# Attention followed by a mixture of attention experts: four of six head pairs' partial sums taken ahead for the projections of the last two batches

## The chip, the cores and the metric

The kernel runs on one core of one Trainium2 chip. The metric is device time in microseconds of one execution, the median of several runs. Before the change three runs gave 306.2, 306.74 and 307.45 us.

A core has engines that work side by side, each on its own queue in order: TensorE (PE: matmuls and transposes; its weight loads are shown as PEld), VectorE (DVE), ScalarE (ACT), GpSimd (POOL) and SyncE (SP, which here issues nearly all DMAs). Matmul results land in PSUM, eight banks of 512 f32 per partition, and another engine has to move them to SBUF.

## What is computed

Two layers follow each other. The first is softmax attention with a soft cap, 8 batches, 12 heads, 448 positions, head size 64:

```
scores = scale * q @ k.T
scores = cap * tanh(scores / cap)        # cap = 30
attn   = softmax(scores)
out    = attn @ v                        # 12 heads side by side: x, 768 columns
```

The second takes x (8 x 448 x 768) and runs four causal attention experts, of which each position uses two:

```
logits = x @ w_gate                      # 4 experts; the best two, softmax over their logits
for e in range(4):
    q, k, v = x @ wq[e], x @ wk[e], x @ wv[e]      # 64 columns each
    a   = softmax(causal(scale * q @ k.T))
    out += weight[e] * (a @ v @ wo[e])   # weight 0 where e is not chosen
```

## The kernel before, in words

**Tiles.** The twelve heads of a batch are six *pairs*; there are 48 pairs (`HP` = 6 to a batch), numbered p = 0 to 47. A pair's scores lie in two PSUM tiles, X (three banks) and Y (two banks). For each pair ScalarE runs three tanh over them (L840: X, Y1, Y2) and then one big exponential in SBUF (L852), and then goes on to the next pair. Of the last batch (batch 7) only the first 320 positions (`W1`) are done pair by pair; the other 128 positions of its six pairs are put together in two more steps, 48 and 49. So there are 50 steps. Batch 7's steps are therefore shorter than the earlier ones.

**From a pair to x.** TensorE multiplies the exponentials with V (L867 and L875 in `pv`), VectorE divides by the row sum (L896, L899, tile xk), and the result is transposed into xT, either by TensorE and a VectorE copy (L920, L929) or, from pair 36 on, by a DMA transpose (`turned`, L395). xT[b] has six parts of 128 rows, one for each pair of the batch.

**The experts of a batch.** When a batch's six parts of xT are there, `b_v` multiplies them with the V and gate weights (L989, 260 columns, four position groups n, six matmuls each, one for each pair), and VectorE copies logits (L998, tile lg) and V (L1001, tile vB). `b_qk` does the same for keys and queries (L1016, two groups of two experts, r = 0 and 1). From the logits GpSimd finds the chosen experts in a chain of small steps (`b_gate`, L1056 to L1069, tile ms) and spreads them as a mask (L1112, tile mB). From batch 4 on (`MD`) the mask is transposed by DMA (tile mT) and VectorE multiplies the queries with it (L1034, tile qm). Each of the two choices s = 0 and 1 then has scores (`b_score`, L1156, in the banks of X), one exponential of 1024 columns on ScalarE (L1165, tile pP), a causal cut on GpSimd (L1175, L1182), a product with V (`b_pv`, L1215, L1228, L1230, tile oB), a sum of both choices on GpSimd (`b_ot`, L1240, tile oS), a transpose, and the output projection (`b_wo`, L1277, copied to ob and stored).

The two exponentials of batch b stand in ScalarE's order in steps 6(b+1)+5 and 6(b+1)+6 (`XOFF` = (5, 6)): behind the big exponential of the step before. For batch 6 these are steps 47 and 48.

**The last batch.** `last` does batch 7's first 320 positions: four groups of six matmuls for k and q (L1379, 320 columns), with the gate's logits in between (L1387), V (L1408), scores and exponentials (L1427, L1437), the product with V (L1465), `normed` and the output projection (L1343). `pv2` (L946 to L973) and `last2` (L1525 to L1583) do the same for the remaining 128 positions, which come from the steps 48 and 49. `gate_tail` has the gate's small operations, among them an exponential of 12 columns on ScalarE (L1508).

**What sets the order.** Nothing is issued as it stands in the text. Each operation is recorded in a graph (`G.op`) with its engine, an estimated duration, what it reads and writes, and for some a due time relative to a ScalarE step. `Graph.solve` then plays the graph through with these estimates and picks for each engine, whenever it is free, the ready operation with the earliest due time, shifted by small random amounts (`SEEDS`, `JIT`); groups that go through PSUM get a bank from the list that they name (`AUX` are three banks of their own, `XB` and `YB` those of X and Y). The result is one fixed order for each engine. ScalarE's tanh and exponentials are a fixed chain (`fixed=True`). `evac` lets the planner choose VectorE or ScalarE for a copy, but ScalarE only once its fixed chain is through. Matmuls of a constant tile (`fill`, `NFILL` and `KEEP`) are put in to keep TensorE busy.

Of the kernel before, what the change touches and what calls it, by code (L numbers as in the profile page):

```python
# [19 lines left out]
LAND = 3.672  # L20
LAND0 = 2.314
FLIGHT = 8
JIT = 1.311
SEEDS = (0, 0, 462, 42, 0, 0, 848, 875, 631, 747, 944, 508, 0, 157, 0, 451, 317, 0, 0, 263, 942, 466, 0, 323, 179, 428, 996, 522, 22, 0, 0, 688, 216, 360, 755, 0, 184, 766, 0, 878, 0, 0, 193, 491, 257, 999, 0, 0, 0, 0, 0, 46, 344, 791, 0, 247, 0, 975, 0, 115, 0, 910, 522, 30, 881, 955, 210, 710, 0, 0, 686, 106, 982, 50, 688, 176, 30, 348)
# [4 lines left out]
KEEPN = 2  # L29
HEAD = 12.0  # L30
# [3 lines left out]
NFILL = 46  # L34
# [19 lines left out]
class Graph:  # L54
# [79 lines left out]
    def solve(self, when, banks, lent):  # L134
# [44 lines left out]
        while len(order) < n:  # L179
            best = None  # L180
            for e, rs in ready.items():
# [8 lines left out]
                def rank(x):  # L190
                    u = x[1]
                    if u.name[:4] == "gexp":
                        return -INF, 0.0, 0
                    d = u.due + lag if u.first or left < TAIL else max(u.due + lag, t0 + 0.148)
                    d -= 7.381 * (u.grp is not None and not u.opens and left >= TAIL)
# [3 lines left out]
                    return d - 9.88 * (u.half == 1 and half == 1), u.due, u.idx  # L199

                near = t0 + (0.022 if left >= TAIL else SWITCH + 0.02)
                t, o = min((x for x in c if x[0] <= near), key=rank)
                early = e == "POOL" and t < HEAD
                if (e in ("PE", "DVE") or early) and not o.first:
                    for t2, u in c:
                        if u.first and u.due + lag < t + o.occ + 0.047 and t2 < t + (
                                o.occ if early else max(SWITCH + 0.01, min(o.occ, 0.25))):
                            t, o = t2, u
                            break
# [66 lines left out]
def kernel(  # L276
# [82 lines left out]
    def bank(g):  # L359
        return BANK[g.bank]  # L360
# [93 lines left out]
    eul = sb("eul", [128, 4, 1], f32)  # L454
    slL = sb("slL", [128, 4, E], f32)
# [371 lines left out]
    late = {}  # L827
# [152 lines left out]

    def b_v(b, ref):
        x = b % 2
        for n in range(4):
            g = Group(AUX + XB, 1.8)
            w = WIN[n]
            for j0 in (0, 2, 4):
                def mm(g=g, w=w, j0=j0):
                    for j in (j0, j0 + 1):
                        nc.tensor.matmul(  # L989
                            bank(g)[:, 0 : E * Dh + E], xT[x][:, j, w : w + 128], wvg[:, j, :],  # L990
                            start=(j == 0), stop=(j == NDC - 1),
                        )

                pe(0, mm, [("xT", x, j) for j in range(NDC)] + [("wvg", e) for e in range(E + 1)],
                   [("vps", b, n)], g, occ=0.22, name=f"v{b}_{n}",
                   due=(ref, 3.171 + 1.4 * n))
            lo = 64 if n == 3 else 0
            dve(0.08, lambda g=g, n=n: nc.vector.tensor_copy(  # L998
                lg[x][:, (n + 1) % 4, :], bank(g)[:, E * Dh : E * Dh + E]),
                [("vps", b, n)], [("lg", x, n)], g)  # L1000
            dve(c_dve(E * Dh), lambda g=g, n=n, lo=lo: nc.vector.tensor_copy(  # L1001
                vB[x][lo:128, n, :, 0:Dh],
                bank(g)[lo:128, 0 : E * Dh].rearrange("p (e d) -> p e d", d=Dh)),
                [("vps", b, n)], [("vB", x, n)], g, name=f"vB{b}")

    def b_qk(b, ref):
        x = b % 2
        for r in range(2):
            for which in "kq":
                g = Group(AUX + XB, 2.4)  # L1010
                w2 = (wq2 if which == "q" else wk2)[r]
                for j in range(NDC):
                    def mm(g=g, w2=w2, j=j, which=which):
                        for o, t in ((0, slice(0, S)),) if which == "k" else (
                                (0, slice(KM, S)), (TL, slice(0, KM))):
                            nc.tensor.matmul(  # L1016
                                bank(g)[:, o : o + t.stop - t.start], w2[:, j, :],
                                xT[x][:, j, t], start=(j == 0 and o == 0), stop=(j == NDC - 1),
                                skip_group_check=True)

                    pe(S, mm, ([("mB", 0), ("mB", 1)] if which == "q" and b >= MD else []) + [("xT", x, i) for i in range(NDC)] + [
                            (f"w{which}2", 2 * r), (f"w{which}2", 2 * r + 1)],
                        [(which, b, r)], g, name=f"{which}{b}_{r}",
                        due=(ref, 22.258 + 3.706 * r + 9.535 * (which == "q")))
                if which == "k":
                    dve(c_dve(S), lambda g=g, r=r: nc.vector.tensor_copy(
                        kB[x][r], bank(g)[:, 0:S]), [("k", b, r)], [("kB", x, r)], g, name=f"kB{b}")
                    continue
                if b < MD:
                    dve(c_dve(S), lambda g=g, r=r: nc.vector.tensor_copy(  # L1030
                        qB[x][r], bank(g)[:, 0:S]), [("q", b, r)], [("qB", x, r)], g, name=f"qB{b}")
                    continue
# [232 lines left out]
    def b_wo(b, ref, off, step=1.0):  # L1265
        x = b % 2
        for n in range(4 if b < LB - 1 else 3):
# [3 lines left out]
            for f in range(2):  # L1271
                g = Group(AUX + XB if b < LB - 1 else AUX, 1.6)
# [91 lines left out]
    def last(ref):  # L1364
# [9 lines left out]
        for r in range(2):  # L1374
            for which in "kq":
                g = Group(ANY, 2.4)
                w_ = (wq2 if which == "q" else wk2)[r]
                for j in range(NDC):
                    pe(W1, lambda g=g, w_=w_, j=j: nc.tensor.matmul(  # L1379
                        bank(g)[:, 0:W1], w_[:, j, :], xT[x][:, j, 0:W1], start=(j == 0),  # L1380
                        stop=(j == NDC - 1), skip_group_check=True),
                        xr + [(f"w{which}2", 2 * r), (f"w{which}2", 2 * r + 1)],
                        [(which, b, r)], g, name=f"{which}L{r}_{j}")
                    if which == "q" and r == 0:
                        def lgt(g=g, j=j):
                            for n in range(3):
                                nc.tensor.matmul(  # L1387
                                    bank(g)[:, W1 + E * n : W1 + E * (n + 1)],
                                    xT[x][:, j, WIN1[n] : WIN1[n] + 128], wvg[:, j, E * Dh :],
                                    start=False, stop=(j == NDC - 1), skip_group_check=True)  # L1390

                        pe(0, lgt, xr + [("wvg", E)], [("q", b, 0)], g, occ=0.09, name="lgL")
# [61 lines left out]
        for n in range(3):  # L1454
# [5 lines left out]
            def mm(g=g, n=n):  # L1460
                for e in range(E):
# [11 lines left out]
                   [(b, 3, "z")]), None, WIN1[n], (ref, 11.607))  # L1473
# [45 lines left out]
    def last2(ref):  # L1519
# [67 lines left out]
        for e in range(E):  # L1587
# [3 lines left out]
               gt2[3][:, 1, 0], W1, (ref, 11.726))  # L1591
# [15 lines left out]
    for p in range(NPV):  # L1607
# [13 lines left out]
        for what in order:  # L1621
            if what == "Y2" and p:
# [4 lines left out]
                xt(p - 1, (ACTS["Y1", p], 4.099))  # L1627
# [91 lines left out]
```

## Time and profile before

| what | value |
|---|---|
| median of three runs | 306.74 us |
| the profiled execution, its own time | 306.68 us |
| its span, first to last instruction | 304.9 us |
| mean granted TensorE clock | 0.996 |
| PE busy | 281.0 us (92%) |
| DVE busy | 213.8 us (70%) |
| ACT busy | 290.5 us (95%) |
| POOL busy | 184.4 us (60%) |
| last tanh or big exponential ends | 285.08 us |

A row of a timeline gives the start in us from the span's beginning, the duration, the engine, the source line, the operation, output <- inputs with their shapes, how many instructions were merged (x3), and in brackets the engine's idle time before it with what ended that. In a merged row of TensorE the time goes from the first start to the last end; matmuls overlap, since the next begins while the one before drains. A due time or an estimate in the code is the planner's, not a measurement.

### The profile page before, as it was taken

What the parts mean: (1) busy time and instruction counts of PE and PEld (TensorE: products, weight loads), DVE (VectorE), ACT (ScalarE), POOL (GpSimd) and SP (SyncE); (2) the same over time, 40 slices, a digit from 0 to 9 for tenths busy, and PEclk for the clock granted to TensorE, in tenths of its full rate; (3) what the DMA queues carried; (4) which work ended last, traced back from release to release, by engine and by line L of the source; (5) the groups of instructions that cost most, each with busy time, mean ns of one, the idle gap of its engine ahead of it and who ended that gap; (6) DMA issues with size and microseconds to landing.
All of it is one profiled execution on the core that took longest, in us unless ns stands there. A gap on an engine that the chain in (4) does not pass through costs nothing.

```text
span 304.9 us, 9009 instructions
## 1 busy us (share of the span) xinstructions
PE 281.0 (92%) x3499; PEld 188.9 (62%) x3499; DVE 213.8 (70%) x646; ACT 290.5 (95%) x245; POOL 184.4 (60%) x515
## 2 busy tenths in 40 slices
PE   8988789999999999999999999989999999999993
PEld 4554456676765776667665677656665666567751
DVE  3344557766777877777876878688876867588783
ACT  5999999999999999999999999999999999999572
POOL 6882253998699586855689473945677312932230
PEclk9999999999999999999999999999999999999998
DMA  6789989998983699769984973259038820655127
GB/s 180 173 202 246 241 200 297 254 248 218 257 199 117 196 260 228 189 180 271 246 217 121 256 210 114 37 155 218 3 69 105 251 53 19 56 149 133 37 113 251
DMA packets 86875, 53.13 MB, mean 174 GB/s; under 512 B 47536, under 2 KB 83120, under 8 KB 86832
## 3 DMA queue, kind: packets, MB, share of 16 engines
q1 hardware_dynamic: 86448, 52.13, 68.5%
q8 instruction: 27, 0.44, 0.7%
q10 hardware_dynamic: 384, 0.43, 0.4%
q14 instruction: 16, 0.13, 0.2%
HBM read 36.19 MB, written 11.01 MB: 155 GB/s over the span
## 4 chain that ended last, share of the span: by engine, by line
ACT 48%; PE 35%; DVE 6%; POOL 5%; issue 3%; DMA 3%; ACTq 0%; POOLq 0%; DVEq 0%
ACT yp L840 25%; ACT yp L852 20%; PE A L875 4%; PE Y L787 4%; PE A L1016 4%; PE X L1156 3%; PE A L1277 3%; PE A L867 2%; PE A L989 2%; ACT pP L1165 2%; DMA vf<-in_v_dram 1%; PE A L691 1%; PE X L787 1%; DMA ktf<-in_k_dram 1%; PE X L797 1%
## 5 line engine op out<-in xcount | busy, mean ns | idle before, releaser
L852 ACT ACTIVATE yp<-yp 128x3136 f16<-128x3136 f16 (+4 forms) x51 | 140.5, 2758 | 0.0
L840 ACT ACTIVATE yp<-Y 128x896 f16<-128x896 f32 (+2 forms) x100 | 97.8, 978 | 1.2 <-PE Y L787 1.2
L840 ACT ACTIVATE yp<-X 128x1344 f16<-128x1344 f32 (+2 forms) x50 | 66.5, 1330 | 0.2
L875 PE MATMUL A<-v,yp 128*128 128x65 f16 x1116 | 55.3, 193 | 0.0
L875 PEld LDWEIGHTS <-yp 128*128 128x128 f16 x1116 | 48.4, 97 | 5.1 <-issue 3.6
L867 PE MATMUL A<-vtz,yp 128*128 128x130 f16 x186 | 41.3, 222 | 5.5 <-ACT yp L852 3.3
L899 DVE TENSOR_TENSOR xk<-A,rca 128x256 f16<-128x256 f32 (+1 forms) x96 | 39.6, 415 | 2.8
L896 DVE RECIPROCAL rca<-A 128x4 f32<-128x4 f32 (+1 forms) x96 | 17.0, 178 | 27.8 <-PE A L875 26.3
L641 POOL CAST q<-qf 112x512 f16<-112x512 f32 x44 | 26.7, 617 | 9.4 <-PE A L691 7.9
L677 POOL CAST v<-vf 128x384 f16<-128x384 f32 x48 | 24.3, 514 | 12.6 <-PE A L875 9.0
L383 DVE COPY ob<-A 128x384 f32<-128x384 f32 (+1 forms) x51 | 27.0, 552 | 4.6 <-PE A L1277 4.1
L867 PEld LDWEIGHTS <-yp 128*128 128x128 f16 x186 | 18.0, 97 | 18.8 <-issue 8.9
L626 POOL CAST k<-kf 128x384 f16<-128x384 f32 x33 | 16.5, 514 | 18.2 <-DMA kf<-in_k_dram 10.6
L787 PE MATMUL Y<-qk 64*128 64x448 f16 x136 | 24.7, 358 | 2.2 <-ACT yp L840 1.9
L1230 DVE SCALAR_TENSOR_TENSOR oB<-A,rcb,mw 128x256 f16<-128x256 f32 x53 | 24.8, 480 | 1.4 <-DVE rcb L1228 0.2
L750 DVE COPY qk<-A 128x960 f16<-128x960 f16 x32 | 20.7, 653 | 6.4 <-PE A L691 6.0
L1277 PE MATMUL A<-wo,oT 128*128 128x384 f16 x108 | 23.9, 326 | 1.1 <-DVE xT L929 0.5
L1215 PE MATMUL A<-vB,pP 128*128 128x260 f16 x134 | 22.1, 274 | 0.9 <-DVE qk L750 0.4
L989 PE MATMUL A<-wvg,xT 128*128 128x260 f16 x168 | 20.8, 274 | 0.2 <-DVE xT L929 0.2
L1016 PE MATMUL A<-xT,wk 128*128 128x448 f16 x84 | 20.0, 353 | 0.3 <-DVE oB L1230 0.2
L1016 PE MATMUL A<-xT,wq 128*128 128x64 f16 (+1 forms) x168 | 20.2, 260 | 0.0
L691 PE MATMUL A<-ident,q 112*128 112x112 f16 x192 | 19.2, 214 | 1.0 <-DVE oB L1230 0.4
(231 smaller groups left out, 582.1 us busy)
## 6 DMA issues: line engine op xcount, KB each, us to landing
qf<-in_q_dram SPq DMA_DIRECT2D x23, 448.0 KB, 6.2
kf<-in_k_dram SPq DMA_DIRECT2D x23, 384.0 KB, 5.4
vf<-in_v_dram SPq DMA_DIRECT2D x23, 384.0 KB, 5.6
out_dram<-ob SPq DMA_DIRECT2D x21, 384.0 KB, 3.4
ktf<-in_k_dram SPq DMA_DIRECT2D x46, 32.0 KB, 4.9
vtf<-in_v_dram SPq DMA_DIRECT2D x46, 32.0 KB, 4.7
out_dram<-ob SPq DMA_DIRECT2D x6, 192.0 KB, 3.1
ob<-in_moe_wv_dram SPq DMA_DIRECT2D x2, 384.0 KB, 4.7
```

Of the source, the lines that this page charges most:

```text
L383: (nc.scalar.copy if o.eng == "ACT" else nc.vector.tensor_copy)(dst(), src())
L641: e(q16[i], qf[s][:, h].rearrange("p h (c d) -> p c h d", c=QC))
L787: nc.tensor.matmul(dst[:, g, o], kT[r, 128 * (c + 1) : 128 * (c + 2)], t[r, qs], start=True, stop=True,)
L840: ACTS[what, p] = act(c_act(n * (b - a)), lambda: nc.scalar.activation(y[:, a:b, 0:n], src[:, 0 : b - a, 0:n], AF.Tanh, scale=isc / capf), ...
L852: act(c_act(n * (b - a), False), lambda a=a, b=b, n=n: nc.scalar.activation(y[:, a:b, 0:n], y[:, a:b, 0:n], AF.Exp, scale=capf), ks, ks, f ...
L867: nc.tensor.matmul(ps[:, n, :, :], y[:, 2 * S + w : 2 * S + w + 128], vtz[u], start=(n == 0), stop=False, skip_group_check=True,)
L875: nc.tensor.matmul(ps[:, n, h, :], y[:, o : o + 128], v16[u][:, h, c, :], start=False, stop=(c == 2), skip_group_check=True,)
L899: dve(c_dve(128 * m), lambda g=g, i=i, rc=rc, m=m: nc.vector.tensor_tensor(xk[p % NXK][:, 2 * i : 2 * i + m, :, :], view(g)[:, 0:m, :, 0:D ...
L989: nc.tensor.matmul(bank(g)[:, 0 : E * Dh + E], xT[x][:, j, w : w + 128], wvg[:, j, :], start=(j == 0), stop=(j == NDC - 1),)
L1016: nc.tensor.matmul(bank(g)[:, o : o + t.stop - t.start], w2[:, j, :], xT[x][:, j, t], start=(j == 0 and o == 0), stop=(j == NDC - 1), skip ...
L1230: dve(c_dve(E * Dh) + 0.06, lambda g=g, k_=k_, n=n: nc.vector.scalar_tensor_tensor(oB[s][:, n, :, :], view(g)[:, :, 0:Dh], rcb[k_][:, 0, : ...
L1277: nc.tensor.matmul(bank(g)[:, 0 : D // 2], oT[x][:, n // 2, r, n % 2, :], wo2[r][:, c0:c1], start=(r == 0), stop=(r == 1),)
```

## The change

For the last two batches, the sums over the first four of the six pairs are formed as soon as these four pairs are there, copied to SBUF as f32, and added again when the sum over the other two pairs is evacuated.

- Batch 6 (`LB - 1`): the new function `b_half`, called in step 40 (6 x 6 + 4, when the pairs 36 to 39 are through), forms partial sums for the four groups of V and logits and for the keys of r = 0. `b_v` and `b_qk` then run over the last two pairs only, and VectorE adds (`plus`) instead of copying. The other three key and query groups of batch 6 stay as they were.
- Batch 7: in `last`, each of the four groups for k and q is split in a group over four pairs (bank from `AUX`) with a copy to SBUF, and a group over two pairs, whose evacuation is an addition on VectorE. The logits' matmuls of the first four pairs stand behind the fifth pair's projection.
- `late`: batch 6's two exponentials stand in steps 46 and 47 instead of 47 and 48.
- Output projections of batch 6 may use X's banks too, and their due times move.
- The planner's constants, seeds and due times are new, and 35 instead of 46 short warm-up matmuls are issued.

```diff
-NFILL = 46
+NFILL = 35
+LDUE = 7.797
+LSTEP = 0.74
+PJ = 4
+PDUE = 2.793
+PSTEP = 11.594
...
-    late = {}
+    late = {LB - 1: (4, 5)}
...
+    def plus(b, key, out, src, part):
+
+        if b < LB - 1 or key not in half:
+            return nc.vector.tensor_copy(out, src)
+        return nc.vector.tensor_tensor(out, src, part(half[key]), ALU.add)
...
+    def b_half(b, ref):
+
+        x = b % 2
+        xr = [("xT", x, j) for j in range(PJ)]
+        for i in range(4):
+            n = (0, 3, 1, 2)[i]
+            g = Group(AUX + XB, 1.8)
+            for j0 in range(0, PJ, 2):
+                pe(0, lambda g=g, n=n, j0=j0: v_mm(g, x, n, range(j0, min(j0 + 2, PJ)), 0, PJ - 1),
...
+            dve(c_dve(E * Dh + E), lambda g=g, n=n: nc.vector.tensor_copy(
+                half["v", n], bank(g)[:, 0 : E * Dh + E]), [("hp", "v", n)], [("half", "v", n)], g,
+                name="hv")
+        for i, (which, r) in enumerate((("k", 0),)):
...
     def b_v(b, ref):
         x = b % 2
+        j1 = PJ if b == LB - 1 else 0
...
         for r in range(2):
             for which in "kq":
-                g = Group(ANY, 2.4)
                 w_ = (wq2 if which == "q" else wk2)[r]
-                for j in range(NDC):
+                h = (which, r)
+                g = Group(AUX, 2.4)
+                for j in range(PJ):
                     pe(W1, lambda g=g, w_=w_, j=j: nc.tensor.matmul(
                         bank(g)[:, 0:W1], w_[:, j, :], xT[x][:, j, 0:W1], start=(j == 0),
+                        stop=(j == PJ - 1), skip_group_check=True),
...
+                dve(c_dve(W1), lambda g=g, h=h: nc.vector.tensor_copy(
+                    halfL[h], bank(g)[:, 0:W1]), [("hpL",) + h],
+                    [("halfL",) + h] + halfL_w[h], g, name=f"h{which}L")
+                g = Group(ANY, 2.4)
+                for j in range(PJ, NDC):
...
-                evac(W1, lambda dst=dst: dst[:, 0:W1], lambda g=g: bank(g)[:, 0:W1],
-                     [(which, b, r)], [(f"{which}B", x, r)], g, name=f"{which}Bl")
+                dve(c_dve(W1), lambda dst=dst, g=g, h=h: nc.vector.tensor_tensor(
+                    dst[:, 0:W1], bank(g)[:, 0:W1], halfL[h], ALU.add),
+                    [(which, b, r), ("halfL",) + h], [(f"{which}B", x, r)], g, name=f"{which}Bl")
...
+                if p == HP * (LB - 1) + PJ:
+                    b_half(LB - 1, ACTS["Y1", p])
...
-                        b_wo(bb, ACTS["Y1", p], *((22.656, 1.8) if bb < LB - 1 else (16.715, 0.5)))
+                        b_wo(bb, ACTS["Y1", p], *((21.59, 1.8) if bb < LB - 1 else (21.884, 0.5)))
```

More of the change, by code (lines that the diff above doesn't have):

```diff
@@ L997, in b_v @@
-            lo = 64 if n == 3 else 0
[L998 to L1004, printed above, removed]
+            hr = [("half", "v", n)] if b == LB - 1 else []
@@ L1010, in b_qk @@
                 g = Group(AUX + XB, 2.4)
-                w2 = (wq2 if which == "q" else wk2)[r]
-                for j in range(NDC):
[L1013 to L1031, printed above, removed]
+                soon = b == LB - 1 and (which, r) in half
```

119 lines of the change are left out of this document (88 added, 31 removed).

## The prediction

> **What bounds the kernel now.** I read the page's head first, then busy time by stretches, then ScalarE's timeline at the end. The columns of a stretch are PE, PEld, DVE, ACT and POOL (busy us, with instruction counts), the granted TensorE clock, the DMA share and GB/s.
>
> ```profile
> span 304.9 us, 9009 instructions
> ...
> 50.00:100.00 50.00, 48.57 (x627) 33.09 (x628) 36.58 (x106) 49.96 (x37) 44.53 (x118) 1.00 0.89 223
> ...
> 270.00:275.00 5.00, 5.00 (x84) 3.66 (x82) 4.03 (x13) 5.00 (x6) 1.36 (x5) 1.00 0.43 124
> 275.00:280.00 5.00, 4.98 (x69) 3.50 (x67) 4.27 (x17) 5.00 (x6) 0.76 (x2) 1.00 0.75 198
> 280.00:285.00 5.00, 4.99 (x78) 3.79 (x77) 4.76 (x21) 5.00 (x5) 2.26 (x2) 1.00 0.18 30
> 285.00:290.00 5.00, 4.94 (x76) 3.80 (x74) 3.62 (x16) 1.74 (x7) 0.36 (x2) 1.00 0.12 26
> 290.00:295.00 5.00, 4.57 (x54) 3.03 (x54) 4.18 (x17) 4.35 (x11) 2.97 (x8) 1.00 0.17 70
> 295.00:300.00 5.00, 4.67 (x51) 2.49 (x47) 4.53 (x16) 3.30 (x9) 0.00 (x0) 1.00 0.65 259
> ```
>
> ```profile
> 264.75 2.24 ACT L852 ACTIVATE yp<-yp 128x2240 f16<-128x2240 f16 x1
> 266.70 0.88 ACT L840 ACTIVATE yp<-Y 128x640 f16<-128x640 f32 x1
> ...
> 268.73 2.27 ACT L852 ACTIVATE yp<-yp 128x2240 f16<-128x2240 f16 x1
> 270.74 1.17 ACT L1165 ACTIVATE pP<-X 128x1024 f16<-128x1024 f32 x1
> ...
> 276.02 1.08 ACT L1165 ACTIVATE pP<-X 128x1024 f16<-128x1024 f32 x1
> ...
> 282.36 0.30 ACT L1508 ACTIVATE gt<-gt 128x12 f32<-128x12 f32 x1
> 282.46 2.62 ACT L852 ACTIVATE yp<-yp 128x1920 f16<-128x1920 f16 x2
> 287.12 0.43 ACT L383 CAST qB<-X0s 128x320 f16<-128x320 f32 x1 [2.04 <-PE X0s L1379]
> ...
> 300.41 0.52 ACTq L1358 DMA_DIRECT2D out_dram<-kf  x1
> ```
>
> The reader sees two stages. As far as 285.08 us (282.46 + 2.62) ScalarE sets the time: 49.96 of 50 us busy in one stretch, 5.00 of 5 from 270 to 285. Work taken from another engine there gives nothing; a wait put before a ScalarE instruction costs its full length. Behind 285.08 comes the tail, 19.8 us to the span's end, in which ScalarE waits (2.04 us for one projection of the last batch). TensorE is full from 270 to 290 and at 4.57 and 4.67 of 5 afterwards, VectorE at 4.18 and 4.53. What leaves TensorE's queue after about 280 us should therefore shorten the tail, unless VectorE is late.
>
> **Term 1: TensorE's work behind the last scores.** The last scores of the attention start at 279.71. I compare the planned queues behind them in both programs.
>
> ```profile
> 278.12 0.64 PE L1215 MATMUL A<-vB,pP 128*128 128x260 f16 x4
> 278.78 0.33 PE L920 MATMUL A<-ident,xk 128*128 128x128 f16 x3
> 278.95 0.27 PE L1215 MATMUL X2s<-vB,pP 128*128 128x260 f16 x1
> ...
> 279.71 0.34 PE L787 MATMUL Y<-qk,kd 64*128 64x128 f16 x6
> ...
> 282.64 0.57 PE L1379 MATMUL A<-xT,wk 128*128 128x320 f16 x3
> ...
> 283.31 0.30 PE L1379 MATMUL A<-xT,wk 128*128 128x320 f16 x1
> ```
>
> One 320-column matmul takes 0.30 from start to end and three take 0.57, so each further one holds the queue (0.57 - 0.30)/2 = 0.135 us; for 260 columns it is (0.64 - 0.27)/3 = 0.12. Before, 24 projections k and q of batch 7 stand behind the last scores; after, 8 do, the other 16 (four pairs in each of four groups) standing in front: -16 x 0.135 = -2.16. But nine matmuls of batch 6's attention times V stand there instead of three (+6 x 0.12 = +0.72), and the three transposes of pair 47, ahead of the scores before (0.33 with their drain, half taken), come behind them (+0.15). Sum: **-1.29**. If VectorE is what the tail waits for, it is 0; if the nine and the transposes fill holes, -2.16. I take -1.29, as TensorE's 4.94 of 5 is nearest to a full queue. All twelve output projections of batch 6 stay in the tail in both queues, so the earlier exponentials relieve nothing there.
>
> Each of the four new half sums costs a VectorE copy of 128x320, and each later evacuation becomes an addition.
>
> ```profile
> 260.53 0.62 DVE L1026 CAST kB<-A 128x448 f16<-128x448 f32 x1
> ...
> 267.74 0.60 DVE L1034 TENSOR_TENSOR qm<-A,mT 128x448 f16<-128x448 f32 x1
> ...
> 287.26 0.49 DVE L383 CAST kB<-X1s 128x320 f16<-128x320 f32 x1
> ```
>
> An operation on two tensors takes 0.60 where a copy of that width takes 0.62: the additions cost what the copies did. The new copies are 4 x 0.49 = 1.96 us and fall before the last scores, in 270 to 285, where VectorE has 15 - (4.03 + 4.27 + 4.76) = 1.94 us left: hidden, with no reserve. Behind that, two V evacuations and one of the last rows' k go to ScalarE and one q evacuation comes back from it. I cost this at 0, and its lower cover is rival 2. Batch 6's five half copies (four of 260, one of 448 columns) fall near 250 us, where ScalarE is the bound; 0, if no score is late.
>
> **Term 2: the small exponential.** The gate's exponential at 282.36 takes 0.10 in front of the last big one at 282.46. After, it stands behind it: **-0.10**.
>
> **Term 3: batch 6's first exponential has a new wait.** Before, it runs at 270.74. After, it stands behind the big exponential that ends at 266.70, four microseconds sooner. It needs scores, these need the masked queries, these a transposed mask, this the gate, and this the logits.
>
> ```profile
> 255.61 0.31 PE L787 MATMUL Y<-qk,kd 64*128 64x320 f16 x2
> ...
> 255.85 0.84 PE L989 MATMUL A<-wvg,xT 128*128 128x260 f16 x6
> ```
>
> ```profile
> 258.57 0.16 DVE L998 COPY lg<-A 128x4 f32<-128x4 f32 x1
> ...
> 264.26 0.42 DVE L899 TENSOR_TENSOR xk<-A,rca 128x256 f16<-128x256 f32 x1
> ...
> 268.46 1.67 DVE L1034 TENSOR_TENSOR qm<-A,mT 128x448 f16<-128x448 f32 x3
> ```
>
> ```profile
> 258.81 0.29 POOL L1056 TENSOR_TENSOR g_c<-lg 128x64 f32<-128x64 f32 x1 [4.09 <-DVE lg L998]
> ```
>
> ```profile
> 263.04 3.92 SPq L395 DMA_TRANSPOSE mT<-mB  x2
> ```
>
> ```profile
> DMA to landing us min/median/max: 4.3/4.5/4.6
> ```
>
> ```profile
> 269.58 1.06 PE L1156 MATMUL X<-qm,kB 128*128 128x256 f16 x18
> ```
>
> In the new TensorE queue the fourth V projection of batch 6 (now two matmuls) stands right behind the scores that started at 255.61, so at 255.85, the place of the row shown. Two matmuls end 0.39 later, at 256.24. In VectorE's queue one normalisation (0.42 and its reciprocal) stands ahead of the logits: they start near 256.5 and GpSimd's first gate step at 256.75 instead of 258.81, 2.06 sooner. From there to the mask's DMA it was 263.04 - 258.81 = 4.23: issue at 260.98. Landing 4.5 later: 265.48. Two multiplications, the second 0.53 behind the first and 0.60 long: 266.6. The first scores may begin on the first of them; all 18 take 1.06: 267.65 to 267.7. ScalarE is free at 266.70: **+1.0** of idle time, and everything up to the last exponential moves with it.
>
> Bounds: with a landing of 4.3, and the first scores overlapped with the second multiplication, +0.6; with 4.6 and a logits copy later by one V evacuation (0.42), +1.5; 0 if the gate gains two more microseconds, for which I see no reason. Behind the waiting multiplication in VectorE's queue stand the normalisations of pairs 44 and 45 and five copies of batch 5's output; they are 1.5 us later than ScalarE's beat would allow, but VectorE was idle before them (rival 3 is the case where this does not suffice).
>
> The Trainium skill's page "DMA: Bandwidth & Descriptors", section "Latency and other measured facts", gives DMA transposes 261 GB/s; the mask is 256 KB, so the estimate from it would be 1.0 us plus the issue. By that price the mask would land over 2 us sooner and term 3 would be 0, which is rival 1; the trace's 4.3 to 4.6 us disagrees, and I go by it.
>
> **What moves elsewhere.** The new seeds and dues reorder the whole queue, loads included. ScalarE's order is the same up to pair 45. I cost this at 0, since before it hid everything (0.04 us of ScalarE idle in 50 to 100), with up to +1 if one load comes late, and not below zero, as ScalarE has nothing left to gain there. Eleven warm-up matmuls fewer are issued, all behind the first scores, where TensorE waits for ScalarE: 0.
>
> **Sum.** The profiled execution took 306.68 us, 1.78 outside its span, and the three runs have a median of 306.74, so no correction is needed. 306.68 - 1.29 - 0.10 + 1.0 = 306.29: **306.3 us**, no change that can be told. A measurement of this kernel tells about 0.5% (1.53 us) from no change.
>
> **Rivals.**
>
> 1. *No wait at batch 6's exponential.* The mask lands in time and the relief stays: 306.68 - 1.29 - 0.10 = 305.3; with the full 2.16 it is 304.4. For it: the chain to the logits loses two thirds of its matmuls. Against it: the row of 255.61 holds back the fourth projection. Chance 0.25.
> 2. *The relief is not had, because VectorE becomes the tail's bound.* Its stretch of 270 to 285 has 1.94 us free and gets 1.96; the evacuations of the last keys and queries then come late and TensorE idles: 306.68 - 0.10 + 1.0 = 307.6. For it: 4.76 of 5 at 280 to 285. Against it: three evacuations go to ScalarE. Chance 0.17.
> 3. *Slower: a second stall behind the first.* The second mask's transpose stands behind the first in the DMA queue; its products free the bank in which pair 45's attention times V starts, and TensorE's queue has the scores of pair 47 behind that. It decides when the second mask lands over 1.2 us later than the first: the two issues together took 3.92 us in the row above, so the second may start up to 2.6 behind. Then 1.4 us are added to the 1.0, and VectorE, late by 2.4, lets no relief through: 306.68 + 2.4 - 0.10 = 309.0. Against it: the earlier row was held up by two other transposes in front. Chance 0.17.
> 4. *It doesn't do what it says*: the moved sums still wait for the last pairs, and the exponential is not sooner in time. The added copies then cost 0 to 0.5: about 307. Chance 0.03; the new queues do show the four partial groups in front.
>
> **How the numbers follow.** The forecast (305.5 to 307.2) has 0.38, rivals 0.25, 0.17, 0.17, 0.03. Faster than 305.2 are about three quarters of rival 1 and a little of the forecast's lower end: 0.21. Slower than 308.3 are rival 3 and the upper end of rival 2: 0.20. Within: 0.59. The range goes from 304.4 (rival 1 with full relief) to 309.0 (rival 3), leaving out some 0.15; the forecast's own is 305.5 to 307.2.
>
> **What would show it.** Term 3: ScalarE idle of about 1.0 us before the first exponential of batch 6, released by the masked scores, with the multiplication before them waiting for the mask's DMA, and GpSimd's first gate step of batch 6 near 256.7. Term 1: the last big exponential ending near 286.0, and from there 18.5 us to the end instead of 19.8. Rival 1: no idle there. Rival 2: VectorE without gaps from 275 to 290 and TensorE waiting for its evacuations. Rival 3: a second gap before the tanh of pair 47. The forecast is wrong if ScalarE shows idle time before 240 us, which no term contains, or if the tail's length stays at 19.8.

## The result, and the profile after

The changed kernel has a median of 305.07 us (six runs, 304.30 to 305.50), the kernel before one of 307.06 beside it (six runs, 306.20 to 307.45). The ratio is 0.9934, 95% interval 0.9916 to 0.9952: 0.66% or 2.0 us faster, and the interval lies wholly below 1. The forecast was 306.3, no change that can be told; rival 1, no wait at batch 6's exponential, gave 305.3.

The head of the page of the changed kernel, and its busy time by stretches (columns as before):

```profile
span 303.4 us, 8986 instructions
...
270.00:275.00 5.00, 5.00 (x74) 3.75 (x73) 3.71 (x14) 4.62 (x5) 1.62 (x6) 1.00 0.61 202
275.00:280.00 5.00, 5.00 (x67) 3.36 (x66) 4.32 (x12) 5.00 (x6) 0.00 (x0) 1.00 0.11 25
280.00:285.00 5.00, 5.00 (x86) 4.21 (x83) 4.93 (x19) 5.00 (x5) 1.76 (x2) 1.00 0.39 121
285.00:290.00 5.00, 4.97 (x74) 3.77 (x73) 4.65 (x22) 2.55 (x10) 0.96 (x2) 1.00 0.23 52
290.00:295.00 5.00, 4.86 (x66) 2.80 (x61) 4.51 (x19) 4.70 (x14) 2.94 (x8) 1.00 0.21 80
295.00:300.00 5.00, 3.55 (x33) 1.86 (x31) 3.41 (x12) 2.83 (x7) 0.00 (x0) 1.00 0.99 383
```

The two stages are the same. From 270 to 285 ScalarE is still full but for 0.38 us; behind it TensorE stays fuller than before in 290 to 295 (4.86 against 4.57) and falls off sooner (3.55 in the last row against 4.67): the tail's work is denser and ends earlier.

The timeline of the changed kernel along the chain of term 3, then ScalarE at the end of its stage, then the end of the kernel:

```profile
256.56 0.29 POOL L1107 TENSOR_TENSOR g_c<-lg 128x64 f32<-128x64 f32 x1 [5.05 <-DVE lg L999]
260.78 2.72 SPq L400 DMA_TRANSPOSE mT<-mB  x2
263.74 0.62 DVE L1085 TENSOR_TENSOR qm<-A,mT 128x448 f16<-128x448 f32 x1 [1.11 <-PE Y L801]
264.48 2.12 ACT L866 ACTIVATE yp<-yp 128x2240 f16<-128x2240 f16 x1
264.62 0.62 DVE L1085 TENSOR_TENSOR qm<-A,mT 128x448 f16<-128x448 f32 x1 [0.25 <-PE A L1011]
265.25 1.08 PE L1207 MATMUL X<-qm,kB 128*128 128x64 f16 x18
266.44 1.07 ACT L1216 ACTIVATE pP<-X 128x1024 f16<-128x1024 f32 x1
...
273.40 1.13 ACT L854 ACTIVATE yp<-X 128x1152 f16<-128x1152 f32 x1 [0.38 <-PE X L801]
...
279.89 0.34 PE L801 MATMUL Y<-qk,kd 64*128 64x128 f16 x6
...
282.49 2.58 ACT L866 ACTIVATE yp<-yp 128x1920 f16<-128x1920 f16 x2
...
297.75 0.82 PE L1394 MATMUL A<-wo,oTL 128*128 128x384 f16 x4
...
299.12 0.53 ACTq L1409 DMA_DIRECT2D out_dram<-kf  x1
```

```profile
DMA to landing us min/median/max: 2.7/2.8/2.9
```

Batch 6's first exponential runs at 266.44 with no bracket behind it: ScalarE waited for nothing. The gate began at 256.56 and the masks were issued at 260.78, but they landed in 2.7 to 2.9 us, not 4.5. The scores end at 266.33 (265.25 + 1.08), 0.11 us before ScalarE is free. The first multiplication, at 263.74, is put down to a score matmul that it does not read; the mask, issued at 260.78, landed just then (263.65) and is the likelier cause.

For the end, the kernel before has this last matmul (its last scores, its last store and its span stand in the prediction):

```profile
298.92 0.81 PE L1343 MATMUL A<-wo,oTL 128*128 128x384 f16 x4
```

That gives the account of the profiled executions (306.68 and 305.08 us). The last scores start 0.18 later (279.71, 279.89). From there to the end of the last matmul TensorE takes 18.68 instead of 20.02: -1.34. From there to the span's end, one copy and a store, 4.8 instead of 5.2: -0.4. Sum -1.6. ScalarE's last big exponential ends where it did (285.08, 285.07), so the whole gain lies in the tail.

### The profile page after: what moved, and what is told of

The parts are those of the page before. It is cut to its first block, busy times and chain, and to the rows that moved or that the text cites. A ratio compares the mean times of both kernels' runs of the same rounds, so it can differ in the third digit from the quotient of the medians.

```text
span 303.4 us, 8986 instructions
## 1 busy us (share of the span) xinstructions
PE 281.0 (93%) x3488; PEld 187.7 (62%) x3488; DVE 218.2 (72%) x653; ACT 290.8 (96%) x247; POOL 184.7 (61%) x515
## 4 chain that ended last, share of the span: by engine, by line
ACT 59%; PE 30%; issue 3%; DMA 3%; DVE 2%; SPq 1%; POOL 1%; POOLq 0%; ACTq 0%
ACT yp L854 29%; ACT yp L866 25%; PE A L1011 4%; ACT pP L1216 4%; PE A L889 3%; PE Y L801 3%; PE A L1328 3%; DMA kf<-in_k_dram 2%; PE A L1003 2%; PE A L1266 2%; PE A L881 2%; PE X L1207 1%; PE A L934 1%; PE X L801 1%; DMA oT<-oS 1%
## 5 line engine op out<-in xcount | busy, mean ns | idle before, releaser
L854 ACT ACTIVATE yp<-Y 128x896 f16<-128x896 f32 (+2 forms) x100 | 99.2, 992 | 1.2 <-PE Y L801 1.2
L913 DVE TENSOR_TENSOR xk<-A,rca 128x256 f16<-128x256 f32 x96 | 39.9, 415 | 3.2
L388 DVE COPY ob<-A 128x384 f32<-128x384 f32 (+1 forms) x48 | 25.2, 551 | 4.7 <-PE A L1328 4.3
L910 DVE RECIPROCAL rca<-A 128x4 f32<-128x4 f32 x96 | 17.0, 178 | 15.3 <-PE A L889 13.9
L1328 PE MATMUL A<-wo,oT 128*128 128x384 f16 x98 | 22.4, 325 | 1.0 <-DMA oT<-oS 0.5
L1291 POOL TENSOR_TENSOR oS<-oB,oB 128x512 f16<-128x512 f16 x14 | 16.0, 1153 | 10.6 <-issue 9.5
L1003 PE MATMUL A<-wvg,xT 128*128 128x260 f16 x168 | 22.1, 274 | 0.4 <-DVE vB L999 0.3
L705 PE MATMUL A<-ident,q 112*128 112x112 f16 x192 | 19.9, 213 | 1.2 <-POOL q L655 1.1
L1226 POOL TENSOR_SCALAR_AFFINE_SELECT pP<-pP 128x384 f16<-128x384 f16 x14 | 7.4, 525 | 20.6 <-ACT pP L1216 20.6
```

What stands on the lines that cost most here:

```text
L388: (nc.scalar.copy if o.eng == "ACT" else nc.vector.tensor_copy)(dst(), src())
L854: ACTS[what, p] = act(c_act(n * (b - a)), lambda: nc.scalar.activation(y[:, a:b, 0:n], src[:, 0 : b - a, 0:n], AF.Tanh, scale=isc / capf), ...
L913: dve(c_dve(128 * m), lambda g=g, i=i, rc=rc, m=m: nc.vector.tensor_tensor(xk[p % NXK][:, 2 * i : 2 * i + m, :, :], view(g)[:, 0:m, :, 0:D ...
L1003: nc.tensor.matmul(bank(g)[:, 0 : E * Dh + E], xT[x][:, j, WIN[n] : WIN[n] + 128], wvg[:, j, :], start=(j == j1), stop=(j == jn),)
L1328: nc.tensor.matmul(bank(g)[:, 0 : D // 2], oT[x][:, n // 2, r, n % 2, :], wo2[r][:, c0:c1], start=(r == 0), stop=(r == 1),)
```

## Experiments

**Which part of the change makes the gain.** Theory T: the four partial sums of batch 7 shorten the tail. Rival L: the earlier exponentials do. Each of the next four kernels is planned anew after its edit, but with the constants, seeds and due times of the kernel that it is taken from. Its loss therefore holds two things, what the edit does and what constants cost that belong to another kernel, and idle time can come in far from the edit. Whether the new constants alone would change the time of the kernel before was not run.

*Exponentials back in their old places.*

```diff
-    late = {LB - 1: (4, 5)}
+    late = {}
```

> The changed kernel with batch 6's two exponentials back in the places they had before (one pair later each); all partial sums kept. Theory T, the gain is TensorE's work taken out of the tail by batch 7's four partial sums (the trace: 18.70 us from the last scores' start to the last matmul's end against 20.04): still 305.1, within 0.5. Rival L, the earlier exponentials make the gain, since batch 6's attention and output leave the tail earlier: 306.4 to 307.0.

308.63 us, ratio to before 1.0059 (1.0038 to 1.0080): slower than both kernels, and outside what either theory expected. The timeline of this kernel:

```profile
274.19 0.78 PE L1207 MATMUL X<-qm,kB 128*128 128x256 f16 x12
...
275.47 1.25 PE L1431 MATMUL A<-xT,wk 128*128 128x320 f16 x8
276.56 0.71 PE L1431 MATMUL A<-xT,wq 128*128 128x320 f16 x4
...
277.82 0.33 PE L1207 MATMUL X<-qm,kB 128*128 128x128 f16 x4
...
278.25 1.02 ACT L1216 ACTIVATE pP<-X 128x1024 f16<-128x1024 f32 x1 [1.56 <-PE X L1207]
```

Twelve matmuls of the new partial sums (L1431) stand in TensorE's queue between the scores of batch 6's second exponential, and ScalarE idles 1.56 us; another 0.43 is lost at the first exponential. In the tail TensorE takes 19.18 from the last scores, 0.5 more than with the earlier exponentials, as 14 matmuls of batch 6's attention stand there instead of 9. The profiled execution loses another 1.8 from its last matmul to the span's end (6.6 instead of 4.8), which was not followed up. So T as stated falls, and L too: in this plan the partial sums cost ScalarE 2.0 us of idle time, more than the 1.3 that they bring in the tail, and the earlier exponentials clear the stretch in which the sums are taken.

*Batch 7 without its partial sums.*

```diff
-                h = (which, r)
-                g = Group(AUX, 2.4)
-                for j in range(PJ):
...
                 g = Group(ANY, 2.4)
-                for j in range(PJ, NDC):
+                for j in range(NDC):
...
-                dve(c_dve(W1), lambda dst=dst, g=g, h=h: nc.vector.tensor_tensor(
-                    dst[:, 0:W1], bank(g)[:, 0:W1], halfL[h], ALU.add),
+                evac(W1, lambda dst=dst: dst[:, 0:W1], lambda g=g: bank(g)[:, 0:W1],
```

> The changed kernel without batch 7's four partial sums: its k and q projections are whole groups of six matmuls again, evacuated by copies; batch 6's partial sums and the earlier exponentials stay. Theory T: the 16 matmuls of 0.135 us are back behind the last scores, 305.1 + 1.3 to 2.2 = 306.4 to 307.2. Rival L: 305.1, within 0.5.

306.18 us, ratio 0.9986 (0.9966 to 1.0005): of the 0.66% there is 0.14% left, within the interval nothing; by the medians 1.1 us are lost, and the interval does not meet that of the changed kernel (0.9916 to 0.9952). From the last scores to the last matmul TensorE takes 19.76 against 18.68, +1.08; the 16 moved matmuls come back, and fewer of batch 6's attention stand beside them. The whole tail, from the last big exponential to the span's end, is 19.75 against 18.29. ScalarE's stage ended 0.9 sooner in this plan (0.6 of that was there in the first 25 us), which hides part of the loss. T is right in this half: given the earlier exponentials and these constants, the partial sums of batch 7 carry most of the gain.

*Batch 6 without its partial sums.*

```diff
-                if p == HP * (LB - 1) + PJ:
-                    b_half(LB - 1, ACTS["Y1", p])
...
-        j1 = PJ if b == LB - 1 else 0
+        j1 = 0
```

> The changed kernel without batch 6's partial sums: V and k projections whole, earlier exponentials and batch 7's partial sums kept. By the forecast's chain the gate's first step goes back from 256.6 to about 258.8 us, the masks' issue to 263.0; with a landing of 2.8 the scores end near 267.7, with 4.5 near 269.5, against ScalarE free at 266.4: idle time of 1.3 to 3.1 before batch 6's first exponential, 306.4 to 308.2. Rival, the planner finds room by itself and the partial sums of batch 6 buy nothing: 305.1.

*The kernel before with the earlier exponentials alone* (the same one-line edit, the other way round):

> The kernel before with the earlier exponentials alone: no partial sums, old constants. Theory T: the gate of batch 6 is not sooner, so batch 6's first exponential waits 1.3 to 3.1 us and the tail keeps its 19.8: 308.1 to 310.1. Rival L: the tail gets shorter by itself, 306.0 or less. Third: the planner hides both, about 307.

311.63 us (ratio 1.0154, 1.0132 to 1.0175) and 321.83 us (1.0486, 1.0463 to 1.0510), both slower than any theory expected. Without the partial sums of batch 6: an idle time far ahead, the gate's first step, a small operation of the gate on VectorE, and batch 6's first exponential. Then the kernel before, its gate and its exponential:

```profile
176.30 1.02 ACT L1216 ACTIVATE pP<-X 128x1024 f16<-128x1024 f32 x1 [1.30 <-POOL kz L645]
...
259.25 0.29 POOL L1107 TENSOR_TENSOR g_c<-lg 128x64 f32<-128x64 f32 x1 [1.87 <-DVE lg L998]
...
267.08 0.18 DVE L1151 RECIPROCAL g_w<-g_w 128x4 f32<-128x4 f32 x1 [1.41 <-POOL g_w L1143]
...
270.10 1.02 ACT L1216 ACTIVATE pP<-X 128x1024 f16<-128x1024 f32 x1 [1.14 <-PE X L1207]
```

```profile
266.12 0.29 POOL L1056 TENSOR_TENSOR g_c<-lg 128x64 f32<-128x64 f32 x1 [7.71 <-DVE lg L998]
...
279.93 1.02 ACT L1165 ACTIVATE pP<-X 128x1024 f16<-128x1024 f32 x1 [9.27 <-PE X L1156]
```

Without batch 6's partial sums the gate comes at 259.25 instead of 256.56, 2.7 us later. But 2.3 of that is not the gate's: ScalarE itself is that late in this plan (the big exponential of 260.50 starts at 262.82), from idle times at exponentials of earlier batches, 0.80 at 105.16 and 1.30 at 176.30, which the edit does not touch. Measured from ScalarE's beat, the start of its big exponentials, the gate is 0.4 later. The exponential then waits 1.14. That this is near the 1.3 of the forecast's chain is chance: the first mask had landed at 266.19, and VectorE stood until 267.08 at a small operation that GpSimd released, in front of the multiplication. Another 3.4 us are lost in the tail (21.7 from the last big exponential to the end, against 18.3), which was not followed up. So this run does not show what batch 6's partial sums bring.

In the kernel before with the earlier exponentials the gate comes at 266.12 and the wait is 9.27; there too ScalarE was late ahead of it, 3.7 us behind the kernel before. In this plan the earlier exponentials alone are a heavy loss. How much of it due times made for the new places would take away was not run.

**Why the mask landed in 2.8 and not 4.5.** The landings of the other two masked batches in the trace of before, batch 4 and then batch 5, could have been read ahead of the result:

```profile
DMA to landing us min/median/max: 2.7/3.1/3.5
```

```profile
DMA to landing us min/median/max: 4.7/4.8/4.9
```

So both prices were there. The row that the forecast used has one thing beside it. A mask is 1,024 packets of 256 bytes; these are the DMA packets of the 0.7 us in which the first half of batch 6's first mask moved (264.2 to 264.9, before; columns are packets, MB, and their time as a share of 16 engines), and then those of the next 1.6 us (264.9 to 266.5).

```profile
q1 hardware_dynamic: 507, 0.13, 463.8%
q8 instruction: 1, 0.02, 14.5%
...
mT<-mB SPq DMA_TRANSPOSE x2, 4.5
```

```profile
q1 hardware_dynamic: 24, 0.01, 3.7%
```

One packet of 16 KB from an instruction queue starts in the same stretch. The mask's packets that start there are under way for 463% of the engines' time (about 100% in full flow: 98.7% from 264.5 to 265.2 in the kernel before with 84 more instructions, below), and behind them the mask all but stands still: 24 packets in 1.6 us. By its volume that queue is TensorE's:

```profile
PE 281.0 (92%) x3499; PEld 188.9 (62%) x3499; DVE 213.8 (70%) x646; ACT 290.5 (95%) x245; POOL 184.4 (60%) x515
...
q8 instruction: 27, 0.44, 0.7%
```

0.44 MB over 2 x 3499 instructions is 63 bytes each, and 27 packets make one in 259 instructions. Such a packet is called a piece here. Theory F: a transpose whose packets meet such a piece lands late. Rival Q: it lands late because two other transposes stand directly ahead of it in the queue, as they did before and not after. The other masks of the same trace go with F: a piece starts 0.5 us behind the issue of batch 4's first mask (landing 3.5) and 1.2 behind that of batch 5's first (4.9), and none near batch 4's second (2.7). The test moves the pieces and nothing else: some of the 42 early warm-up matmuls of 512 columns (pairs 1 to 7, far ahead of everything here) are cut in two or four, which adds TensorE instructions; the planner still sees one operation each, so the order stays.

```diff
-                    pe(512, lambda g=g: nc.tensor.matmul(
-                        bank(g)[:, 0:512], warm[:, 0:128], warm[:, 0:512], start=True, stop=True),
+                    pe(512, lambda g=g, p=p, k=2: [nc.tensor.matmul(
+                        bank(g)[:, i : i + 512 // k], warm[:, 0:128], warm[:, i : i + 512 // k],
+                        start=True, stop=True) for i in range(0, 512, 512 // k)],
```

*The kernel before with 84 more instructions (k = 2):*

> The kernel before, with the 84 more instructions: the piece that arrived at 265.8 us, in the flight of batch 6's masks (issued 263.04 and 264.36, landed in 4.6 and 4.3), moves to about 262.4, ahead of them; two pair transposes stand in front of the masks as before. Theory F: the masks land in 2.7 to 3.3 us; time unchanged, about 307.0, as no exponential waits for them there. Rival Q: 4.3 to 4.6 as before.

307.04 us, one run. The packets of 264.4 to 267.0, in which both masks moved:

```profile
q1 hardware_dynamic: 2106, 0.52, 89.3%
...
mT<-mB SPq DMA_TRANSPOSE x2, 2.8
```

No instruction packet there, no stuck packets, landing 2.7 to 2.8 with the two transposes still in front. The piece now starts at 260.65, and the first of those two transposes, which it meets, lands in 4.0 us instead of 2.3. Q falls. Batch 5's masks, 4.7 to 4.9 before, landed in 2.7 to 2.8 as well.

*The changed kernel with 84 more (k = 2) and 108 more (k = 4 for pair 7, else 2), and the control with 252 more (k = 4):*

> The changed kernel with each of its 42 early 512-column warm-up matmuls cut into two of 256: 84 more TensorE instructions (matmul and weight load each) far ahead of everything disputed, same order otherwise. TensorE's instruction stream comes in 16 KB pieces, one in about 256 instructions (0.44 MB for 6,976 matmuls and loads); 84 more move the piece that arrived at 266.7 us to about 264.4. Theory F, a transpose whose flight meets such a piece lands late: the second mask of batch 6 (issued 262.15) lands in 4.0 to 4.8 us instead of 2.7, the first still in 2.8 to 2.9; ScalarE has no new idle time, time 305.1. Rival Q, a transpose lands late when others stand directly ahead of it in the queue: the order is the same, so both land in 2.7 to 2.9; time 305.1.

> As the run with 84 more instructions, but six of the 42 matmuls are cut into four: 108 more, and the piece of instructions moves to about 263.0, into the flight of the first mask of batch 6 (issued 260.78). Theory F: the first mask lands in 4.0 to 4.8 us, near 265.3; the multiplications end near 266.4, the scores near 267.4, and ScalarE idles 0.6 to 1.0 before batch 6's first exponential, as the forecast had it: 305.1 + 0.8 = 305.9. Rival Q: landing 2.7 to 2.9, no idle time, 305.1.

> Control: all 42 warm-up matmuls cut into four, 252 more instructions, which is about one whole piece, so the pieces arrive where they did. Theory F: both masks of batch 6 land in 2.7 to 2.9 us, no idle time, 305.1. If the added instructions themselves cost something, or delay the transposes by another way than the place of the pieces, it shows here: over 305.5 or a landing over 3.5. Rival Q: 2.7 to 2.9 too.

304.43 us (ratio 0.9922, 0.9897 to 0.9948), 304.38 (0.9914, 0.9891 to 0.9936) and 305.24 (0.9943, 0.9922 to 0.9964); landings 2.7 to 2.9, 2.7 to 2.8, 2.8 to 3.1. The first two did not test what they were made for. Their expectations took a slow trickle of packets at 266.7 in the changed kernel for the piece, but the trickle follows it; the piece itself came at 265.1, and 84 more instructions brought it to 260.4, ahead of the masks' data. The control put it back at 265.0, as one period should.

*48 more (k = 2 for pairs 1 to 4) and 60 more (pairs 1 to 5), set from the right place:*

> The changed kernel with 24 of its early warm-up matmuls cut in two: 48 more TensorE instructions. In the run with 84 more, the 16 KB piece of TensorE's instructions that came at 265.1 us (by the single packet of the instruction queue) came at 260.4, ahead of the masks' data, so that run did not test what it was made for. 48 more should bring it to about 262.4, while the first mask's packets move (262.0 to 263.2). Theory F, packets of a transpose that share the DMA engines with such a piece get stuck until it is through: the first mask of batch 6 lands in 4.2 to 4.8 us instead of 2.8, near 265.3, and ScalarE idles 0.6 to 1.0 before batch 6's first exponential; 0.8 longer than the kernels of the same order, 305.2 to 305.9. Rival Q, the transposes ahead in the queue decide: landing 2.7 to 2.9, no idle time, 304.4 to 305.1.

> As the run with 48 more, but 60 more: the piece at about 261.7, just ahead of the first mask's data or at their start. Theory F: if the piece starts at 262.0 or later, landing 4.2 to 4.8 and idle time 0.6 to 1.0 as above; if it starts over a microsecond ahead of the data, 2.7 to 2.9 and none. Rival Q: 2.7 to 2.9.

305.37 us (ratio 0.9959, 0.9939 to 0.9979) and 305.60 (0.9960, 0.9941 to 0.9980). With 48 more, the packets of 262.6 to 263.7, and the timeline:

```profile
q1 hardware_dynamic: 561, 0.14, 174.8%
q8 instruction: 1, 0.02, 6.5%
...
mT<-mB SPq DMA_TRANSPOSE x1, 3.8
```

```profile
265.02 1.16 DVE L1085 TENSOR_TENSOR qm<-A,mT 128x448 f16<-128x448 f32 x2 [2.61 <-DMA mT<-mB]
267.35 1.02 ACT L1216 ACTIVATE pP<-X 128x1024 f16<-128x1024 f32 x1 [0.99 <-PE X L1207]
```

The piece falls among the masks' packets, the masks land in 4.4 and 3.8 us, VectorE waits 2.61 us for them, and ScalarE idles 0.99 before batch 6's first exponential: the stall of the forecast, made by 48 added instructions over 200 us earlier. With 60 more the piece starts at 263.1, 1.0 behind the first mask's issue at 262.16 (that execution ran 1.4 us late by then, 0.7 of it from its first load); landings are 4.2 and 3.8 and the idle time 0.76. By the medians both kernels are 0.9 to 1.2 us slower than those with 84 and 108 more, whose order is the same; their intervals overlap with that of 84 more and not with that of 108 more.

The fourteen traces of this case have 84 mask transposes. The 21 with a piece starting 0.4 to 2.25 us behind the issue landed in 3.4 to 4.9 us; the 47 with none from 1 us ahead of the issue to the landing took 2.7 to 3.2, but for one of 3.35. Pieces nearer to the issue or to the landing, the other 16, went both ways. Theory F is shown as far as cause and effect go; how the piece holds up the others' packets is not.

**What sets the tail.** The forecast said TensorE, unless VectorE is late. Two kernels load one engine each, without a new dependence: the first matmul of each of the last four k and q projections five times instead of once (16 useless matmuls), or each of the four additions behind them twice.

```diff
-                    pe(W1, lambda g=g, w_=w_, j=j: nc.tensor.matmul(
+                    pe(W1, lambda g=g, w_=w_, j=j: [nc.tensor.matmul(
                         bank(g)[:, 0:W1], w_[:, j, :], xT[x][:, j, 0:W1], start=(j == PJ),
-                        stop=(j == NDC - 1), skip_group_check=True),
+                        stop=(j == NDC - 1), skip_group_check=True)
+                        for _ in range(5 if j == PJ else 1)],
```

> The changed kernel with the first matmul of each of the four last k and q projections issued five times instead of once: 16 useless matmuls of 320 columns behind the last scores, as many as the partial sums took away there, with no other dependence changed. Theory T, TensorE's queue sets the tail: 16 x 0.135 = 2.2 more, 306.4 to 307.3, tail 19.6 to 20.5 instead of 18.3. Rival V, VectorE sets it: 305.1 to 305.6.

```diff
-                dve(c_dve(W1), lambda dst=dst, g=g, h=h: nc.vector.tensor_tensor(
-                    dst[:, 0:W1], bank(g)[:, 0:W1], halfL[h], ALU.add),
+                dve(c_dve(W1), lambda dst=dst, g=g, h=h: [nc.vector.tensor_tensor(
+                    dst[:, 0:W1], bank(g)[:, 0:W1], halfL[h], ALU.add) for _ in range(2)],
```

> The changed kernel with each of the four additions that evacuate the last k and q written twice: 4 x 0.48 = 1.9 us more of VectorE in the tail, nothing else changed. Theory T: at most a part shows, as the additions release the next TensorE work: 305.1 to 306.0. Rival V: the full 1.9, 307.0.

307.20 us (ratio 1.0002, 0.9981 to 1.0024) and 306.94 us (1.0004, 0.9985 to 1.0024): by the medians 2.1 and 1.9 more, so each load shows at about its full price (16 x 0.135 = 2.2 and 4 x 0.48 = 1.9), and each by itself undoes the gain. In the traces the stretch from the last scores to the last matmul grows from 18.68 to 20.6 and 20.8. Neither theory alone is right. The stretch of 285 to 290 with more TensorE work, then with more VectorE work, and then three of the latter's TensorE rows:

```profile
285.00:290.00 5.00, 5.00 (x75) 4.33 (x73) 3.48 (x16) 1.38 (x5) 0.63 (x1) 1.00 0.19 42
```

```profile
285.00:290.00 5.00, 3.67 (x53) 2.91 (x51) 4.65 (x19) 1.59 (x6) 0.55 (x1) 1.00 0.23 52
```

```profile
285.71 0.27 PE L1593 MATMUL A<-xT,wk 128*128 128x128 f16 x2 [0.48 <-DVE xT L987]
...
287.21 0.49 PE L1603 MATMUL A<-wvg,xT 128*128 128x260 f16 x3 [0.42 <-DVE kB L1463]
...
288.94 0.29 PE L1495 MATMUL X2s<-qB,kB 64*128 64x320 f16 x1 [0.36 <-DVE qB L1463]
```

With more matmuls VectorE goes slack (3.48 against 4.65), with more additions TensorE does (3.67 against 4.97, its waits ended by VectorE). At 285 to 290 the path runs through both in turn: projection, addition, scores.

## Why the prediction was right and where it was wrong

The time lies in the range, but the likeliest case did not happen: no change was forecast, and a gain of 0.66% clear of noise came. The range held it because it was drawn wide enough for rival 1, not because the sum came out. By its own steps:

1. **The bound.** Two stages, as read. "VectorE is late" was the wrong form of the question for the tail: both engines are on the path there.
2. **Term 1, -1.29.** Right in size: TensorE's stretch from the last scores to its last matmul shrank by 1.34. That the two agree to 0.05 is closer than the pieces allow: 16 matmuls put back lengthened that stretch by 1.9, where the sum priced 2.16. The additions cost what the copies did, as assumed (0.46 to 0.48 us each against 0.46 to 0.49); the run with double additions shows that this zero mattered. The four half copies, which were to fill VectorE's last 1.94 us of 270 to 285, left it as busy as before (12.96 against 13.06), as small operations of batch 7's gate, among others, moved behind 285; in 285 to 290 it rose from 3.62 to 4.65. Wrong was "the earlier exponentials relieve nothing there": without them that stretch is 0.5 longer and the partial sums hold up the second exponential's scores by 1.56.
3. **Term 2, -0.10.** The small exponential went behind the big one, and ScalarE's stage ended at 285.07 with 0.38 of new idle time in it; the start of batch 6's first exponential had been 0.26 ahead of the old beat (266.44 against 266.70). The three add up to the unchanged end. The 0.26 comes from the new order earlier in the kernel and was not followed up.
4. **Term 3, +1.0: the step that failed is "Landing 4.5 later: 265.48".** All before it held in time: gate 256.56 (forecast 256.75), issue 260.78 (260.98). That it is batch 6's partial sums that made the gate sooner is argued in the forecast and not shown by the run without them. The landing was 2.7 to 2.9, because no piece of TensorE's instructions met the mask. Where one was made to (48 more instructions, landings of 4.4 and 3.8), the 1.0 came true to 0.99. I priced the transpose from one of three batches of the same trace, and called it the trace's price. Against the estimate of 1.0 us plus the issue (1.2 to 1.4 in these rows), worked out from the bandwidth that the Trainium skill's page "DMA: Bandwidth & Descriptors", section "Latency and other measured facts", gives for a non-contiguous middle dimension, the changed kernel shows 2.7 to 2.9 undisturbed: between that and my row, and near enough to the page that rival 1 follows.
5. **What moves elsewhere, 0.** The 0.38 at 273.40 has no term. In the changed kernel a piece met two transposes behind the masks (the packets of 265.0 to 265.7, and the landings of transposes issued by then). TensorE waited for the second, which brings batch 5's attention to its output projection. The projection's first row is shown in the changed kernel and then in the one with 84 more instructions, where that transpose landed in 2.3:

```profile
q8 instruction: 1, 0.02, 14.9%
...
xT<-xk SPq DMA_TRANSPOSE x1, 4.3
oT<-oS SPq DMA_TRANSPOSE x1, 3.3
```

```profile
269.00 0.82 PE L1328 MATMUL A<-wo,oT 128*128 128x384 f16 x4 [0.47 <-DMA oT<-oS]
```

```profile
268.54 0.82 PE L1328 MATMUL A<-wo,oT 128*128 128x384 f16 x4
```

   From this row to the scores for which ScalarE waits at 273.40 both kernels take 4.02 us (to 273.02 and 272.56), so the lateness is carried along. In the control and in the run with double additions a piece meets the same two transposes; the second lands in 3.4 us, and the idle times are 0.23 and 0.45. Where it lands in 2.3 (84, 108, 48 and 60 more) or in 3.2 (16 more matmuls, landed at 268.54 instead of 268.95) there is none. The kernels with 84 and 108 more, which lose neither this nor the 1.0, are 0.6 to 0.7 faster than the changed kernel by the medians, though their intervals overlap with its own. The 0.4 at the last copy and store had no term either: the last copy took 0.48 on ScalarE instead of 0.56 on VectorE, and the store landed about 0.3 sooner.
6. **Rivals.** Rival 1 is what happened, near its time (305.3); that they agree to 0.2 is in part luck, as the 0.38, the 0.4 and the 0.26 were in no sum. Rival 2's premise, that VectorE has no reserve, is right behind 285, where double additions show in full, but the changed kernel's own evacuations let the relief through. Rival 3's condition, as it was written, was met: the second mask landed 1.35 us behind the first (265.00, 263.65). But both landed so early that no idle time stood before the tanh of pair 47; the one at 273.40 stands before step 48's. Rival 4 did not occur.

## What to carry to other kernels

Before a duration from one row is put on a path, look at every instance of that operation in the trace, and where they differ by two thirds, find what stands beside the slow ones. A chain with 0.1 us to spare that ends in a DMA can be lost or won by the number of instructions issued long before it. When two edits of one change are each a loss alone, as in the plans here, test them one at a time and together before crediting either. And before the loss of a kernel with one part taken out is read as what the part is worth, see how much of it was there before the part begins: here 2.3 of 6.6 us.

## What was not expected of the hardware

TensorE's instructions arrive in pieces of 16 KB, one in about 259 instructions (27 packets for 6,998 in the kernel before, 0.44 MB). When one falls among the packets of a transpose from SBUF to SBUF, that transpose lands late, a mask's in 3.4 to 4.9 us instead of 2.7 to 3.2, with its packets' time at 463% of the engines' in the stretch quoted. The Trainium skill's page "Runtime: NRT & Kernel Launch", section "Instruction fetch mechanics", says that instructions are refilled in blocks of 16 KiB or 256 instructions by a DMA queue of the sequencer's own, at a cost that is mostly hidden: the trace agrees on the size, but the cost is not hidden from the transposes. No run here shows whether TensorE itself waits for a piece. Kernels with one and the same order of work, which differ in the number of early instructions alone, had medians from 304.38 to 305.60 us.
